# Decoding w_out by ScalarE's product and scaling it by row sums, with a new order of the first batches and of the last tiles

## The chip, the cores and the metric

The kernel runs on one core of one Trainium2 chip. The metric is the time on the device in microseconds (us). A core has TensorE (PE in the profile; PEld is its weight load), VectorE (DVE), ScalarE (ACT), GpSimd (POOL) and SyncE (SP), which here only issues DMAs. Every engine works through its own instructions in program order.

## The reference

There are 8 batches of 8 heads, 576 positions and 64 columns per head, with 32 memory slots per head:

```
a      = softmax(phi over the sequence)
k_m    = a^T k ;  v_m = a^T v                       # 32 memory rows per head
x      = softmax(q k_m^T / 8) v_m                   # 4608 tokens x 512
g      = s * relu(x @ w_in)^2 + b                   # 512 -> 2048
x      = g @ w_out                                  # 2048 -> 512
h      = x @ w_in2                                  # 512 -> 1024
solu   = h * softmax(h)
out    = (solu - mean) / sqrt(var + 1e-6) * g_ln @ w_out2
```

`w_in`, `w_out` and the two second-layer weights arrive as float64. The kernel reads each number as two 32-bit words and makes the float32 itself: three exponent bits of the high word are dropped, the mantissa is moved up by three bits, and the top three bits of the low word are put below it. Products run on TensorE in pairs of float16 parts (hi and lo, three passes), so each tensor needs a power-of-two scale that keeps the hi part in range.

## The kernel before, in words

The work of batch 0, all decoding and splitting of the first-layer weights, and the start of batch 1 are issued in an order written out by hand, the string `FIRST`. Each word is a step: a name, and after the dot its indices. The same order holds on each engine for the instructions that the step puts there, so the string sets what stands behind what on DVE, ACT, POOL, PE and the SP queue. After it a loop runs batches 1 to 7 (gemm1, gemm2, with the next batch's attention in between), and a last loop runs the second layer over 36 tiles of 128 tokens.

The steps that matter here are these. `w_in` and `w_out` come in eight pieces each (chunk c, half x), of 128x1024 numbers. `Lw` and `Lo` load a piece. `Ai` and `Ao` (line 228) let ACT write the absolute value of the high words to the destination. `Bi` and `Bo` (line 238) are a DVE pass that raises each value to at least 2^-15 and writes the row's maximum out as its accumulator. `Ci` and `Co` are two DVE instructions: a shift with a mask (line 254), and a scalar_tensor_tensor that puts two high bits back (line 245). The low bits are put in either by DVE alone (`PiX`, `PoX`, line 1094), or by POOL (`Pi`, `Po`, line 251) after ACT (`LiA`, `LoA`, line 233) or DVE (`LiD`, `LoD`, line 235) has shifted the low word.

For each of the four chunks of `w_out` the row maxima become one scale: `om` reduces them on DVE, `oad` puts them on a diagonal (DVE, line 170), `oap` multiplies it by ones on PE, `oa` reduces that on DVE (line 180), and `os` makes the power of two. The product of `oap`, like those of `vap` and `map`, takes one of the two PSUM tiles with the tag "y", the ones that gemm2's `ya` and `yb` write. Then `xh` (ACT) and `xl` (DVE, line 280), or `xhP` (two ACT instructions) and `xlP` (POOL, line 1163), write the hi and lo parts. `ya.jd` and `yb.jd` are the two halves of gemm2 of batch 0 (block j, output chunk d; 24 products each).

`g.jp` is gemm1 of batch 0 (12 products for two of the 16 blocks of d_ff), `gr` its relu on ACT (line 953). Its square is done by ACT (`gq`, line 978) or POOL (`gqP`, line 980), the hi part by ACT (`gh`, line 970) or DVE (`ghD`, a cast), the lo part by DVE or POOL (`gl`, `glP`, line 985). `s0` to `s6` and `sT` are the scores of the attention; of these `s5` is a DVE subtraction and `s5P` the same on POOL. Batch 1's queries are loaded (`Lq`) into the space in which the decoded `w_out` pieces lay (`wt_s`), so they wait for the last `xl` or `xlP` that reads it. `qa` and `qs` find their scale (lines 274 and 746), `qh` and `ql` split them, `qT` and `mT` transpose them by DMA, and then PE can run `s0.10` (line 780).

In the last loop one round takes gemm3 of tile i (`tile_mm`, line 1335), the solu of tile i with the float16 parts of tile i-1 (`tile_rest`), and gemm4 of tile i-3 (line 1417). gemm4 needs `lt`, a DMA transpose of the tile's normalised values. The result goes out in two DMAs per tile where a tile crosses a column group (line 1427).

## Time and profile before

| | us |
|---|---|
| median of 3 runs | 1139.3 (1137.97 to 1140.17) |
| the profiled execution, its own time | 1138.68 |
| the profiled execution, span of its instructions | 1136.9 |

| engine | busy us | share of the span | instructions |
|---|---|---|---|
| PE | 1060.9 | 93% | 8208 |
| PEld | 691.5 | 61% | 8208 |
| DVE | 804.7 | 71% | 1551 |
| ACT | 517.8 | 46% | 745 |
| POOL | 242.2 | 21% | 181 |

All times in the profile come from that one execution and count from the start of its span. A busy share is an average over stages that have different limits, so it has to be read stage by stage. An instruction's time includes what it spends waiting inside the engine after it has started.

### The profile page before, as it was taken

How to read it: one execution, taken by the hardware profiler on the slowest of the kernel's cores; microseconds unless marked ns; L12 is line 12 of the kernel's file. 1: busy time of each engine (PE TensorE's matmuls, PEld its weight loads, DVE VectorE, ACT ScalarE, POOL GpSimd, SP SyncE). 2: the span in 40 equal slices, each digit the busy share in tenths (PEclk: the TensorE clock that was granted, in tenths of full speed). 3: DMA queues.
4: the chain of work that ended last, by engine and by line, in shares of the span. 5: the costliest groups of instructions: out<-in, count | busy, mean ns of one | idle time of the engine just before them, and what ended most of it. 6: DMA issues, size and time to landing. Idle time of an engine off the chain costs nothing.

```text
span 1136.9 us, 20489 instructions
## 1 busy us (share of the span) xinstructions
PE 1060.9 (93%) x8208; PEld 691.5 (61%) x8208; DVE 804.7 (71%) x1551; ACT 517.8 (46%) x745; POOL 242.2 (21%) x181
## 2 busy tenths in 40 slices
PE   0676799998999999999999999999999999999997
...
DVE  5989977776976776777777675647666666676662
...
GB/s 290 274 142 211 36 80 102 124 217 119 95 186 71 121 166 59 153 134 83 161 142 95 82 26 172 60 47 98 111 101 91 106 109 101 91 108 106 83 64 100
DMA packets 219488, 134.00 MB, mean 118 GB/s; under 512 B 144896, under 2 KB 207616, under 8 KB 219392
## 3 DMA queue, kind: packets, MB, share of 16 engines
...
q0 software_dynamic: 96, 0.01, 0.0%
...
## 4 chain that ended last, share of the span: by engine, by line
PE 69%; DVE 4%; DMA 3%; ACT 2%; SPq 1%; issue 1%; POOL 0%; POOLq 0%; ACTq 0%
PE y L1002 24%; PE hp L1335 16%; PE y L1417 15%; PE hp L942 10%; PE wp L634 2%; PE kp L438 1%; DMA work<-in_moe_w_out_dram 1%; PE sp L780 1%; DVE g L985 1%; DVE wt_s L280 0%; DMA w_in_t<-wt_s 0%; DMA kv_s<-in_k_dram 0%; DMA lt<-nat 0%; SPq L335 0%; DMA qt_s<-work 0%
## 5 line engine op out<-in xcount | busy, mean ns | idle before, releaser
L1002 PE MATMUL y<-g,w_out 128*128 128x288 f16 (+1 forms) x2880 | 366.0, 287 | 5.3 <-DVE first L180 5.3
L1002 PEld LDWEIGHTS <-w_out 128*128 128x128 f16 x3072 | 298.2, 98 | 98.6 <-issue 18.6
L942 PE MATMUL hp<-aT,vwt 128*128 128x288 f16 x1536 | 198.5, 290 | 7.5 <-ACT r L953 4.1
L1417 PE MATMUL y<-w_t,lt 128*128 128x512 f16 x864 | 192.0, 379 | 1.8 <-DMA lt<-nat 1.8
L1335 PE MATMUL hp<-w_t,xs 128*128 128x512 f16 x864 | 192.2, 379 | 0.0
L942 PEld LDWEIGHTS <-vwt 128*128 128x128 f16 x1536 | 151.5, 99 | 51.3 <-issue 9.3
L1417 PEld LDWEIGHTS <-lt 128*128 128x128 f16 x864 | 84.4, 98 | 103.8 <-DMA lt<-nat 2.2
L1335 PEld LDWEIGHTS <-xs 128*128 128x128 f16 x864 | 84.5, 98 | 101.4
L1379 POOL TENSOR_TENSOR rstd<-ve,nhalf 128x1 f32<-128x1 f32 x36 | 52.7, 1464 | 335.8 <-DVE mv L1377 335.8
L1349 DVE TENSOR_REDUCE hmx<-hp 128x1 f32<-128x1024 f32 x36 | 44.1, 1224 | 86.6 <-PE hp L1335 86.6
L277 ACT ACTIVATE xs<-xt,xsc 128x512 f16<-128x512 f32 x36 | 25.9, 720 | 151.0 <-PE hp L1335 129.6
L1019 ACT ACTIVATE x<-y,bcol,cs 128x288 f32<-128x288 f32 x64 | 37.5, 586 | 122.7 <-PE y L1002 101.5
L985 DVE TENSOR_TENSOR g<-r,g 128x576 f16<-128x576 f32 x115 | 88.9, 773 | 6.3 <-POOL r L980 2.5
L978 ACT ACTIVATE r<-r 128x576 f32<-128x576 f32 x118 | 80.6, 683 | 19.4 <-DVE g L985 15.2
L953 ACT ACTIVATE r<-hp 128x576 f32<-128x576 f32 x120 | 77.1, 643 | 13.2 <-PE hp L942 5.7
L274 DVE TENSOR_REDUCE xmx<-x 128x1 f32<-128x288 f32 x64 | 28.7, 448 | 54.1 <-ACT x L1019 53.4
L928 DVE CAST g<-r 128x576 f16<-128x576 f32 x112 | 51.4, 459 | 19.4 <-ACT r L978 19.4
L1356 ACT ACTIVATE e<-hp,nm,xiv 128x1024 f32<-128x1024 f32 x36 | 43.3, 1203 | 46.5 <-DVE nm L1351 46.5
L856 POOL TENSOR_TENSOR e<-e,ssm 96x512 f32<-96x512 f32 x21 | 22.0, 1046 | 186.0 <-DVE ssm L851 183.9
L1425 ACT ACTIVATE o<-y,io 128x512 f32<-128x512 f32 x36 | 24.8, 689 | 51.6 <-issue 43.2
L1393 DVE TENSOR_TENSOR nat<-so,nat 128x1024 f16<-128x1024 f32 x36 | 43.7, 1215 | 5.4 <-ACT nat L1388 5.4
L1372 DVE BATCH_NORM_STATS2 bs<-so 128x6 f32<-128x512 f32 x72 | 46.3, 685 | 1.2
...
## 6 DMA issues: line engine op xcount, KB each, us to landing
...
```

The costliest lines, as they stand in the source:

```text
L928: nc.vector.tensor_copy(out=g_of(n, j, 0)[:, 2 * fp:2 * fp + 2, 0:BLK], in_=gt["r2", j, fp])
L942: nc.tensor.matmul(out=hp[:, u, 0:BLK], lhsT=vt[:, pw, R, f * 128:(f + 1) * 128], rhs=aT[:, CJ * j:CJ * (j + 1), pa, R, :], start=(x == 0) ...
L953: nc.scalar.activation(out=r, in_=gt.pop(("h", j, fp))[:, :, 0:BLK], func=ACTF.Relu, scale=scale)
L978: nc.scalar.activation(out=r2, in_=r, func=ACTF.Square)
L985: (nc.vector if eng == "D" else nc.gpsimd).tensor_tensor(out=g_of(n, j, 1)[:, fs, 0:BLK], in0=gt.pop(("r2", j, fp)), in1=g_of(n, j, 0)[:, ...
L1002: nc.tensor.matmul(out=y[:, 0:w], lhsT=w_out_t[d][:, pw, f, :], rhs=g_of(n, j, pg)[:, f, 0:w], start=(x == 0), stop=(x == len(steps) - 1),)
L1335: nc.tensor.matmul(out=hp[:, a, :], lhsT=xs[:, px, kk, :], rhs=wt[:, pw, kk, a * 512:(a + 1) * 512], start=(kk == 0 and px == 0 and pw == ...
L1349: nc.vector.tensor_reduce(out=mx, in_=hv, op=ALU.max, axis=AX)
L1372: nc.vector.bn_stats(out=bs[:, a, :], in_=so[:, a * 512:(a + 1) * 512])
L1379: nc.gpsimd.tensor_tensor(out=rstd, in0=ve, in1=nhalf, op=ALU.pow)
L1393: nc.vector.tensor_tensor(out=nat[:, 1, :], in0=so, in1=nat[:, 0, :], op=ALU.subtract)
L1417: nc.tensor.matmul(out=y[:, 0:DM], lhsT=lt[:, pl, f, :], rhs=wt[:, pw, f, :], start=(x == 0), stop=(x == len(steps) - 1),)
```

## The change

Four things are changed. First, `w_out` is decoded in another way. `Ao` is now a product on ACT, the high word read as float32 times 2^-112, which keeps the sign and moves the exponent so that a plain shift by three (first instruction of `Co`) leaves the right one; the second instruction of `Co` puts the sign back. [...] Second, `Bo` is no longer a DVE pass: it is an ACT pass over the decoded piece that writes the sum of absolute values of each row as its accumulator, with the used-up high words as its output. The scale is made from the largest of four such sums (two chunks at a time), so `om`, `oad`, `oap`, `oa` and `os` exist twice instead of four times, and `os` no longer decodes the maximum but copies the inverse scale to two columns. Third, `FIRST` is a new order, in which some steps also run on another engine: 4 of the 8 pieces of `w_in` get their low bits by `PiX` (2 before), one of the others by `LiD`; six `ghD` replace one; `gl` is 7 (5 before) and `glP` 9 (11); `gq` 8 (6) and `gqP` 8 (10); `s5` 1 (4) and `s5P` 5 (2). Fourth, in the last loop gemm3 and the solu of the last tile are issued one gemm4 earlier, and the second output DMA of the last tile is issued by ACT's queue instead of SP's.

```diff
+REBIAS = 2.0 ** -112
 FIRST = """
-Lw.01 Lphi.0 Lw.10 Ai.10 phm.0 pht.0 Lw.00 phd.0 Ai.00 Lw.11 pho.0 Bi.10 Lw.30 phb.0 Ci.10 Bi.00 Ai.01 Lw.20 Ai.11
-Lkv.00 LiA.10 Pi.10 Lkv.02 Bi.01 LiA.30 Lkv.01 Bi.11 phe.0 Ci.11 LiA.11 Ai.20 LiA.20 km.00 Ci.00 Ci.01 Lkv.03 Ai.30
-Lw.31 Bi.30 Lw.21 PiX.00 km.01 Bi.20 im0 ks.00 Ci.30 Ci.20 PiX.01 Lq.01 ks.01 LiA.31 Lq.02 Lq.03 Pi.11 Lq.00 Pi.30
-Ai.31 ko.00 ko.01 Bi.31 vb.0 ia0d mm.0 qm.01 Ai.21 vad.0 mv.0 vap.0 Bi.21 Pi.20 LiA.21 qo.01 ia0p va.0 Lphi.1 im
-Ci.31 iad qm.02 mk.0 qm.03 Ci.21 qm.00 phm.1 qo.02 qo.03 ia0 qo.00 iap s0.00 Lo.01 s1.00 s0.01 ia s2.00 Ao.01 pht.1
-Pi.31 s0.02 vs0 s3.00 s1.01 phd.1 s2.01 s3.01 Lo.10 s6P.00 iv s4.00 Lo.00 s6P.01 vm.00 s5.00 vh.00 vm.01 s4.01 s1.02
-s5P.01 sT.00 vl.00 vh.01 pho.1 vl.01 Pi.21 s2.02 sT.01 Ao.00 Lo.11 phb.1 Lo.20 vs.0 vm.03 vh.03 vm.02 Bo.00 vh.02
-vl.03 g.03 Lkv.11 vl.02 s3.02 Bo.01 Lkv.10 g.01 Ao.11 om.0 LoA.10 s6P.02 Ao.10 gr.01 gh.01 Co.01 gr.03 g.07 gqP.03
-Bo.11 gqP.01 g.06 phe.1 gh.03 gl.01 gr.07 glP.03 gqP.07 gr.06 gh.07 km.10 g.05 gq.06 Co.00 gh.06 Co.11 ks.10 s4.02
-glP.07 gr.05 PoX.01 gh.05 gqP.05 g.02 s5.02 oad.0 Lkv.12 Bo.10 sT.02 oap.0 ko.10 gr.02 Lkv.13 oa.0 g.00 os.0 om.1
-gl.05 gr.00 Co.10 gh.02 PoX.00 oad.1 gh.00 xh.00 xh.01 g.11 oap.1 gl.06 oa.1 xl.00 gqP.02 Lo.21 km.11 gq.00 gr.11
-g.13 Ao.20 LoD.11 os.1 ks.11 xl.01 Po.11 Lo.30 gh.11 Lkv.22 Lphi.2 Lkv.21 Ao.21 Po.10 Bo.20 ko.11 Bo.21 om.2 glP.02
-Co.21 vb.1 gr.13 glP.00 g.10 gh.13 gqP.13 g.04 g.16 vad.1 xhP.11 xh.10 gq.11 Lo.31 glP.13 oad.2 oap.2 gr.10 gr.04
-Co.20 xl.10 PoX.20 g.14 glP.11 xlP.11 gh.04 vap.1 gh.10 gq.04 gqP.10 oa.2 ya.01 PoX.21 Ao.30 glP.04 os.2 Ao.31 gr.16
...
+Lw.01 Lw.20 Lphi.0 Lw.10 phm.0 Ai.20 Lkv.00 pht.0 Ai.01 Bi.20 Lw.00 Ai.10 Bi.01 phd.0 pho.0 phb.0 Bi.10 Ci.20 Ci.10
+phe.0 Lw.11 Ci.01 Lw.30 LiA.10 Ai.11 Ai.00 Bi.11 Lkv.02 Pi.10 Bi.00 im0 Lkv.01 Lkv.03 km.00 km.01 Ai.30 Lq.02 ks.01
+Lw.31 Lq.03 Lq.00 Ci.11 ks.00 LiD.11 PiX.01 Bi.30 PiX.20 Lq.01 qm.02 ko.00 Ai.31 ko.01 qo.02 Ci.00 Lphi.1 Ci.30
+Lw.21 Lkv.10 qm.03 qo.03 mm.0 mv.0 qm.00 Bi.31 vb.0 ia0d qo.00 Lo.01 mk.0 qm.01 qo.01 phm.1 s0.01 vad.0 ia0p LiA.00
+s1.01 Ai.21 vap.0 s2.01 Bi.21 Pi.11 s0.00 s3.01 Pi.00 s1.00 va.0 pht.1 ia0 s2.00 s0.02 s6P.01 Lo.00 phd.1 im s4.01
+s5P.01 s3.00 vs0 vm.01 s6P.00 vm.00 Ci.21 iad sT.01 LiA.21 iap s4.00 s5P.00 vh.01 vh.00 s1.02 s2.02 vl.01 ia Ao.00
+pho.1 sT.00 Pi.21 LoA.01 vl.00 phb.1 vm.02 iv Lkv.11 s3.02 Ao.01 vs.0 Lo.11 s6P.02 PiX.30 g.02 vh.02 g.00 gr.02
+vl.02 s4.02 gqP.02 ghD.02 gr.00 Lo.10 Ci.31 gh.00 Co.01 s5.02 Ao.11 sT.02 gq.00 PiX.31 g.03 g.05 gr.03 glP.02 Co.00
+Co.11 gqP.03 Po.01 phe.1 km.10 gl.00 gh.03 g.04 gl.03 gr.05 gq.05 ks.10 Ao.10 ko.10 ghD.05 LoD.11 Po.11 gr.04 g.11
+Lkv.12 Bo.00 gl.05 Lkv.13 Co.10 PoX.10 gr.11 Bo.01 Bo.11 Bo.10 om.0 g.14 vm.03 oad.0 km.11 gh.04 gqP.04 Lo.21 Lo.30
+glP.04 vh.03 PoX.00 oap.0 oa.0 gr.14 gh.14 g.01 gq.11 os.0 gh.11 gqP.14 ks.11 vl.03 xh.01 g.07 ko.11 g.13 gl.11
+xhP.00 gr.01 xh.10 gq.01 xl.10 g.06 xl.01 gh.01 gr.07 xlP.00 gh.07 gl.01 glP.14 g.16 gr.13 LoD.30 gqP.07 Lkv.22
+Lo.31 vb.1 vad.1 Ao.21 vap.1 Ao.30 gq.13 xh.11 Co.30 Lo.20 g.12 ghD.13 gl.07 xl.11 glP.13 Ao.20 Co.21 Ao.31 gr.06
+Po.30 gr.16 mb.1 gqP.16 g.17 mad.1 gq.06 map.1 Bo.30 Co.31 Bo.21 Bo.31 g.10 gh.16 ghD.06 Co.20 Bo.20 om.1 va.1 oad.1
+Lphi.2 oap.1 ma.1 glP.06 oa.1 os.1 PoX.21 gr.12 glP.16 PoX.20 gqP.12 xhP.20 ya.01 xh.21 ya.00 PoX.31 xh.30 xhP.31
+xlP.20 xl.30 yb.01 xlP.31 Lq.10 gr.10 g.15 cb.1 gh.10 yb.00 ghD.12 xl.21 yo.01 glP.12 qa.10 ym.01 phm.2 vs.1 gr.17
+gq.10 cb.0 pha.2 yo.00 Lq.12 gh.17 Lq.11 ya.02 ym.00 ya.03 Lq.13 qa.13 qa.12 yb.02 qa.11 qs.1 yd.01 qh.11 yd.00
+qh.10 ms.1 cb.2 mm.1 mv.1 mh.1 gr.15 yb.03 ql.10 yo.02 ql.11 qT.11 gqP.15 qT.10 ym.02 cb.3 yo.03 glP.10 vm.11 qh.12
+ghD.15 ml.1 gq.17 ym.03 glP.17 qh.13 ql.12 ya.11 gl.15 qT.12 phbP.2 vm.10 vh.11 ql.13 vh.10 yb.11 vl.11 yo.11 qT.13
+mT.1 ya.13 s0.10 Lkv.20 vl.10 ym.11 yb.13 sc.10 s0.11 yd.03 s1.10 ya.10 vm.12 s2.10 sc.11 s3.10 yd.02 yo.13 s6.10
...
 """
@@ -255,6 +257,22 @@
             out=out_, in0=in_, scalar1=3, scalar2=0x3FFFFFF8,
             op0=ALU.logical_shift_left, op1=ALU.bitwise_and,
         )
+
+
+
+    def decode_rebias(dst, raw):
+        nc.scalar.activation(out=dst, in_=raw[:, :, :, 1].bitcast(FP32), func=ACTF.Copy, scale=REBIAS)
+
+    def decode_shift(dst, raw):
+        di = dst.bitcast(I32)
+        nc.vector.tensor_scalar(out=di, in0=di, scalar1=3, scalar2=None, op0=ALU.logical_shift_left)
+        nc.vector.scalar_tensor_tensor(
+            out=di, in0=raw[:, :, :, 1], scalar=-0x80000000, in1=di, op0=ALU.bitwise_and, op1=ALU.bitwise_or,
+        )
+
+
+    def decode_sum(dst, raw, sm):
+        nc.scalar.activation(out=raw[:, :, :, 1].bitcast(FP32), in_=dst, func=ACTF.Abs, accum_out=sm)
 
     def word_max(pk):
 
@@ -1066,27 +1084,31 @@
             return w_in_dst(c, x), raw_t["in", c, x]
         return words(wt_t[c, x]), raw_t["out", c, x]
 
+    def piece_max(c, x):
+        if "i" not in pk_t:
+            pk_t["i"] = st.tile([128, 8], FP32, tag="pk8", name="pk", bufs=2)
+        decode_max(piece("i", c, x)[0], pk_t["i"][:, 2 * c + x:2 * c + x + 1])
+
+    def piece_sum(c, x):
+        if c // 2 not in pk_t:
+            pk_t[c // 2] = st.tile([128, 4], FP32, tag="pk4", name="pk", bufs=2)
+        col = 2 * (c % 2) + x
+        decode_sum(*piece("o", c, x), pk_t[c // 2][:, col:col + 1])
+
     def piece_abs(w, c, x):
         if w == "o":
             at = (2 * c + x) % 4
             wt_t[c, x] = wt_s[:, at] if at < 3 else flat(kv_s[:, 2])[:, 0:1024]
-        decode_abs(*piece(w, c, x))
+        (decode_abs if w == "i" else decode_rebias)(*piece(w, c, x))
 
     def piece_low(w, c, x, eng):
         decode_low(raw_t["in" if w == "i" else "out", c, x], eng)
 
-    def piece_max(w, c, x):
-        key, col, n = ("i", 2 * c + x, 8) if w == "i" else (c, x, 2)
-        if key not in pk_t:
-            pk_t[key] = st.tile([128, n], FP32, tag=f"pk{n}", name="pk", bufs=2)
-        decode_max(piece(w, c, x)[0], pk_t[key][:, col:col + 1])
-
     def piece_bits(w, c, x):
-        decode_bits(*piece(w, c, x))
+        (decode_bits if w == "i" else decode_shift)(*piece(w, c, x))
 
     def piece_add(w, c, x):
         decode_add(*piece(w, c, x))
-        raw_t.pop(("in" if w == "i" else "out", c, x))
 
 
     def piece_or(w, c, x):
@@ -1095,7 +1117,6 @@
             out=dst.bitcast(I32), in0=raw[:, :, :, 0], scalar=29, in1=dst.bitcast(I32),
             op0=ALU.logical_shift_right, op1=ALU.bitwise_or,
         )
-        raw_t.pop(("in" if w == "i" else "out", c, x))
 
     def w_max(key):
         pk_t["m", key] = word_max(pk_t[key] if key == "i" else pk_t.pop(key))
@@ -1138,14 +1159,14 @@
         nc.vector.tensor_scalar(out=s22, in0=sb[:, 0:1], scalar1=2.0 ** 22, scalar2=None, op0=ALU.mult)
 
     def w_out_scale(d):
-        mx = st.tile([128, 1], FP32, tag="wmx", name="wmx")
-        word_value(pk_t.pop(("m", d)), mx)
-        pk_t["s", d] = pow2_scale(mx, iw[:, d:d + 1], "wsc")
+        inv = st.tile([128, 1], FP32, tag="winv", name="winv")
+        pk_t["s", d] = pow2_scale(pk_t.pop(("m", d)), inv, "wsc")
+        nc.vector.tensor_copy(out=iw[:, 2 * d:2 * d + 2], in_=inv.to_broadcast([128, 2]))
 
     def w_out_ops(d, x):
         sl = slice(8 * x, 8 * x + 8)
         t = wt_t[d, x].rearrange("p (k d) -> p k d", k=8)
-        return w_out_t[d][:, 0, sl], w_out_t[d][:, 1, sl], t, pk_t["s", d]
+        return w_out_t[d][:, 0, sl], w_out_t[d][:, 1, sl], t, pk_t["s", d // 2]
 
     def w_out_hi(d, x, eng):
         hi, lo, t, sc = w_out_ops(d, x)
@@ -1423,8 +1444,9 @@
             )
         o = pools_b["o"].tile([128, DM], FP32, tag="o", name="o")
         nc.scalar.activation(out=o, in_=y[:, 0:DM], func=ACTF.Copy, scale=io2[:, 0:1])
-        for off, n, bb, c, p in runs(i * 128, 128):
-            nc.sync.dma_start(out=out_v[bb, c, p:p + n, :], in_=o[off:off + n, :])
+        for x, (off, n, bb, c, p) in enumerate(runs(i * 128, 128)):
+            eng = nc.scalar if i == NTILE - 1 and x else nc.sync
+            eng.dma_start(out=out_v[bb, c, p:p + n, :], in_=o[off:off + n, :])
 
 
     def load_w_in0(f, kp):
@@ -1460,7 +1482,7 @@
         "Ai": lambda c, x: piece_abs("i", c, x), "Ao": lambda c, x: piece_abs("o", c, x),
         "LiA": lambda c, x: piece_low("i", c, x, "A"), "LoA": lambda c, x: piece_low("o", c, x, "A"),
         "LiD": lambda c, x: piece_low("i", c, x, "D"), "LoD": lambda c, x: piece_low("o", c, x, "D"),
-        "Bi": lambda c, x: piece_max("i", c, x), "Bo": lambda c, x: piece_max("o", c, x),
+        "Bi": piece_max, "Bo": piece_sum,
         "Ci": lambda c, x: piece_bits("i", c, x), "Co": lambda c, x: piece_bits("o", c, x),
         "Pi": lambda c, x: piece_add("i", c, x), "Po": lambda c, x: piece_add("o", c, x),
         "PiX": lambda c, x: piece_or("i", c, x), "PoX": lambda c, x: piece_or("o", c, x),
@@ -1503,15 +1525,13 @@
         def tile_rest(i):
 
 
-            if i < NTILE:
-                solu_1(i, *h3_t.pop(i))
-            if 1 <= i <= NTILE:
+            solu_1(i, *h3_t.pop(i))
+            if i:
                 solu_3(i - 1)
             if i == NTILE - 1:
                 solu_4(i - 1)
-            if i < NTILE:
-                solu_2(i)
-            if 1 <= i <= NTILE and i != NTILE - 1:
+            solu_2(i)
+            if i and i != NTILE - 1:
                 solu_4(i - 1)
 
         h3_t = {}
@@ -1543,17 +1563,25 @@
                     x_max(n // 2)
                     xal_t[n // 2] = all_max(xal_t[n // 2], "xal")
 
+
         for i in range(2, NTILE + 3):
-            if 3 <= i < NTILE:
+            if 3 <= i < NTILE - 1:
                 tile_mm(i)
             if i == 6:
                 x_max(3)
                 xal_t[3] = mm_max_put(xal_t[3])
             if i == 9:
                 xal_t[3] = mm_max(xal_t[3])
-            tile_rest(i)
+            if i < NTILE - 1:
+                tile_rest(i)
+            if i == NTILE - 2:
+                tile_mm(i + 1)
+                tile_rest(i + 1)
             if i >= 3:
                 gemm4(i - 3)
+            if i == NTILE - 1:
+                solu_3(i)
+                solu_4(i)
 
 
 # ---- launch: one core; inputs and outputs as the reference has them ----
```

## Rows read from the trace of the kernel before

**Rows 1.** The page's 40 slices of the span (28.4 us each), busy tenths of PE and DVE.

```profile
PE   0676799998999999999999999999999999999997
DVE  5989977776976776777777675647666666676662
```

**Rows 2.** Windows: start:end, length, busy time of PE, PEld, DVE, ACT, POOL, granted clock.

```profile
11.10:122.20 111.10, 61.76 (x668) 42.89 (x669) 104.93 (x167) 60.37 (x75) 51.21 (x27) 0.88 0.79 215
122.30:136.60 14.30, 14.27 (x96) 10.44 (x96) 14.02 (x23) 6.24 (x8) 8.30 (x5) 0.83 0.08 22
136.60:144.10 7.50, 5.23 (x31) 3.60 (x30) 7.36 (x15) 0.98 (x2) 4.24 (x3) 0.79 0.19 59
```

**Rows 3.** Timeline of PE: start, length, line, count, in brackets idle time and releaser.

```profile
122.33 14.46 PE L1002 MATMUL y<-g,w_out 128*128 128x289 f16 x96 [5.28 <-DVE first L180]
...
136.62 1.63 PE L942 MATMUL hp<-aT,vwt 128*128 128x288 f16 x12
140.53 0.46 PE L175 MATMUL mp<-first 128*128 128x128 f32 x2 [2.27 <-DVE first L170]
...
144.06 3.27 PE L1002 MATMUL y<-g,w_out 128*128 128x289 f16 x24
...
169.83 0.86 PE L780 MATMUL sp<-work 128*96 128x64 f16 x16 [1.07 <-DMA work<-work]
```

**Rows 4.** DVE instructions by line and form until 122.2 us: busy, mean ns, idle before.

```profile
L238 DVE TENSOR_SCALAR_CACHE_REDUCE w_in_t<-w_in_t 128x1024 f32<-128x1024 f32 x8 | 9.6, 1213 | 0.2 <-ACT w_in_t L228 0.2
...
L238 DVE TENSOR_SCALAR_CACHE_REDUCE wt_s<-wt_s 128x1024 f32<-128x1024 f32 x5 | 6.0, 1197 | 0.0
L254 DVE TENSOR_SCALAR w_in_t<-w_in_t 128x1024 int32<-128x1024 int32 x8 | 5.7, 718 | 0.0
...
L245 DVE SCALAR_TENSOR_TENSOR w_in_t<-raw_g,w_in_t 128x1024 int32<-128x1024 int32 x2 | 2.5, 1225 | 0.1
...
L1094 DVE SCALAR_TENSOR_TENSOR w_in_t<-raw_v,w_in_t 128x1024 int32<-128x1024 int32 x2 | 2.4, 1214 | 0.0
```

**Rows 5.** The page's costliest groups over the whole span: two that FIRST uses too.

```profile
L985 DVE TENSOR_TENSOR g<-r,g 128x576 f16<-128x576 f32 x115 | 88.9, 773 | 6.3 <-POOL r L980 2.5
...
L928 DVE CAST g<-r 128x576 f16<-128x576 f32 x112 | 51.4, 459 | 19.4 <-ACT r L978 19.4
```

**Rows 6.** Timeline of DVE, single instructions of the first 160 us.

```profile
11.09 0.69 DVE L360 TENSOR_TENSOR t<-phi_sb 96x512 f32<-96x512 f32 x1 [9.46 <-DMA phi_sb<-in_phi_dram]
...
22.99 0.96 DVE L254 TENSOR_SCALAR w_in_t<-w_in_t 128x1024 int32<-128x1024 int32 x1
...
25.85 3.31 DVE L245 SCALAR_TENSOR_TENSOR w_in_t<-raw_v,w_in_t 128x1024 int32<-128x1024 int32 x1
...
119.92 2.16 DVE L1094 SCALAR_TENSOR_TENSOR wt_s<-w_out,wt_s 128x1024 int32<-128x1024 int32 x1
122.00 0.28 DVE L180 TENSOR_REDUCE first<-mp 128x1 f32<-128x128 f32 x1
...
153.42 0.14 DVE L746 TENSOR_REDUCE qm<-qmx 96x1 f32<-96x4 f32 x1
```

**Rows 7.** Timeline of POOL beside the third of these.

```profile
25.34 2.73 POOL L251 TENSOR_TENSOR w_in_t<-w_in_t,raw_g 128x1024 int32<-128x1024 int32 x1 [1.94 <-ACT raw_g L233]
```

**Rows 8.** Timeline of ACT: two first passes over loaded pieces, and an accumulator read-out.

```profile
13.64 1.12 ACT L228 ACTIVATE w_in_t<-raw_g 128x1024 f32<-128x1024 f32 x1 [11.63 <-DMA raw_g<-in_moe_w_in_dram]
...
26.05 1.13 ACT L228 ACTIVATE w_in_t<-raw 128x1024 f32<-128x1024 f32 x1 [1.13 <-DMA raw<-in_moe_w_in_dram]
...
1070.83 0.19 ACT L1356 ACTIVATION_READ_ACCUMULATOR e<-hp,nm,xiv 128x1 f32 x1
```

**Rows 9.** Timelines of PE, DVE and SP's queue at the end.

```profile
1109.40 15.70 PE L1417 MATMUL y<-w_t,lt 128*128 128x512 f16 x72
1126.86 5.35 PE L1417 MATMUL y<-w_t,lt 128*128 128x512 f16 x24 [1.76 <-DMA lt<-nat]
...
1109.60 1.22 DVE L1349 TENSOR_REDUCE hmx<-hp 128x1 f32<-128x1024 f32 x1 [2.63 <-PE hp L1335]
...
1133.01 0.79 SPq L1427 DMA_DIRECT2D out_dram<-o  x2
```

12 lines of the change are left out of this document (3 added, 9 removed).

## The prediction, on record before the changed kernel ran

> **What bounds the kernel now.** I read the page's slices first: from slice 6 on PE is full to the end, so the 0.9 ms of batches and second layer can only get shorter by less PE work, and the change takes none away there. Lost time lies in the first five slices, where DVE is the full row and PE the one with holes [rows 1]. The windows say the same in numbers: from 11.1 to 122.2 us DVE is busy for 104.9 of 111.1 us, PE for 61.8, ACT for 60.4, POOL for 51.2; up to 144.1 DVE stays full and PE runs at a granted clock near 0.8 [rows 2]. Third the timeline of PE: gemm2 (`ya.01`) starts at 122.33 when a DVE reduction, `oa.2`, has read one of the two "y" tiles of PSUM; the last hole that DVE makes is the 2.27 us ahead of 140.53; at 144.06 `ya.02` starts, and from there PE has work behind it, but for 1.07 us at `s0.10`, which waits for a DMA transpose [rows 3]. So the head is a DVE stage that ends at a gate, and what the change is worth there is how much sooner PE comes to the state it now has at 144.06. Last the end: PE waits 1.76 us for the last tile's transpose before the last gemm4, and two output DMAs are then issued one behind the other [rows 9].
>
> **The gate moves.** In the new order `ya.01` stands behind `map.1` and `oap.1`, so its "y" tile is free when DVE has done `ma.1`. All eight `Co` and all row sums come before that; in the old order six `Co` did. I therefore count DVE's work ahead of `oa.2` (old) and of `ma.1` (new).
>
> Less: six `Bo` passes of 1.2 us [rows 4], 7.2. More: two `Co`, each a 0.7 us shift and a 1.2 us merge [rows 4], 3.8; one merge of low bits in sum (`PiX` 2 to 4, `PoX` 3 to 2), 1.2; two shifts of low words (`LiD`, `LoD`: 1 to 3), taken at the 0.7 of the other shift, 1.4; four `ghD` at 0.46 [rows 5], 1.8; three `gl` at 0.77, 2.3. One `s5` and half a dozen instructions of 0.14 to 0.28 [rows 6] go in sum with one scale chain less, about 1.5, an estimate. Sum: -7.2 + 3.8 + 1.2 + 1.4 + 1.8 + 2.3 - 1.5 = +1.8 us. The gate has more DVE work before it, not less; the two `Bo` and the work left out behind it (over all of `FIRST` DVE loses two more `Bo` and a second scale chain) come back only after the gate.
>
> **The start.** `phm.0` is DVE's first step of weight and waited for phi until 11.09 [rows 6]. phi stood second in SP's queue, behind one 1 MB piece; now it stands third, behind two. The piece that stood right behind phi came at 13.64, 2.55 us later [rows 8]; the seventh transfer came at 26.05, five pieces behind phi, 3.0 us each. I take +2.6, ends +2.0 and +3.0. What DVE does in the order after that (`Bi.20`, `Bi.01`) has its data by then: these two pieces are now ahead of phi.
>
> **POOL beside DVE.** The merge that starts at 25.85 takes 3.31 us where the same form takes 1.2, and ends 1.1 us after POOL's add from 25.34 to 28.07: it waited for POOL's instruction to end [rows 6, 7, 4]. 18 DVE instructions before the gate are lengthened like this, the first at 22.99 (0.96 for 0.69), the last at 119.92 (2.16 for 1.21), in sum by 20 us. With 51.2 us of POOL that is 0.39 us per us. The passes of line 238 are not among them: 8 and 5 of them average 1.21 and 1.20 [rows 4]. The new order has 23 POOL instructions ahead of the gate for 26, which alone gives 20 x 23/26 = 17.7; but six of the fourteen passes beside which POOL ran for nothing are gone. POOL was busy 46% of the stage [rows 2], so 7.2 us of passes covered 3.3 us of it. 17.7 + 3.3 x 0.78 (2.1 lost in 2.73 of POOL, as at 25.85) = 20.3: no change. Ends: 17.7, and 0.78 x 45 us of POOL = 35. I stay at 20, the mean of the 18.
>
> The Trainium skill, page "SBUF — State Buffer", section "Who interferes with whom", says that DVE and GpSimd share a pair of ports as an exclusive lock, that a `tensor_scalar` which also writes out its accumulator does not take it, and that a plain one, or one with two inputs in SBUF, can. By that rule the change removes just those DVE instructions that were free of POOL; the trace agrees (1.20 and 1.21 beside 3.31). By the rule all 3.3 us would turn into waiting, and the gate would be 0.7 us later than by my sum.
>
> **ACT.** Eight sums come to ACT. A pass over a piece takes 1.12 and the read-out of an accumulator 0.19 [rows 8]: 1.3 us each, and three `LiA` and five `gh` go. ACT has 51 us free before the gate [rows 2], so the sum costs nothing; what can cost is its order. Two places: `xl.10` on DVE waits for `xh.10`, which stands behind `xh.01`, the two instructions of `xhP.00` and `gr.01`, some 5.0 us after `os.0`, while DVE has about 2.6 us of other work: 2.4 us of stall. And `om.1` needs `Bo.20`, which needs the last `Co`: 1.3 us at least, 3.7 if `Bo.31` and `gh.16` are still ahead of it. Behind both everything on DVE is queued, and PE behind that. Together 2.4 + 1.5 = 3.9, of which part falls into time that POOL's lock costs anyway; of the 6.2 us of old idle time [rows 2] I expect 2.3 to go (the new order does DVE work where it waited for squares). Net +1.6, ends -2.5 and +5.
>
> **The sum at the head.** Gate: 122.3 + 1.8 + 2.6 + 0 + 1.6 = 128.3. Behind it the four halves `ya.01`, `ya.00`, `yb.01`, `yb.00` took 14.3 us at clock 0.83 [rows 2, 3]; at the 3.0 or so of a half at 144.06 they would take 12. I take 13.2. But between 136.6 and 144.06 PE did two `g` blocks and two small products and stood idle for 2.27; in the new order these are done before the gate. So `ya.02` comes at 141.5 instead of 144.06: -2.5. It has to find its data: `xlP.20` is done some 10 to 11 us after the gate, in time. Next late is `s0.10`: the chain from `qs` (153.42) to it (169.83) took 16.4 us [rows 6, 3], through six DMA transposes and ACT. In the new order I reckon `qs` at about 152, so `s0.10` can run at about 168.4 and PE gets there at about 168. It fits, with nothing to spare.
>
> **The end.** gemm3 of the last tile ends one gemm4 (15.70/3 = 5.2) sooner, at about 1104.4. Its chain from there to the transposed tile took 1126.86 - 1109.60 = 17.3; DVE is still at the solu of the tile before for some 2.5 us more. 1124.2, and PE is through the others at 1109.40 + 15.6 = 1125.0: the wait of 1.76 goes, ends 0 and -1.8. The second output DMA no longer stands behind the first: half of 0.79 [rows 9], -0.4, ends 0 and -0.4. Together -2.2.
>
> **Sum.** -2.5 - 2.2 = -4.7 us against the profiled execution's own 1138.68 (span 1136.9 and 1.8 around it): 1134.0. The median of the runs is 0.6 above that execution: 1134.6.
>
> **Rivals.** (a) *DVE is starved or blocked more*: the price of POOL rises to 0.6 us per us, since merges and shifts now follow each other without a free pass between. Place: DVE between `vl.00` and `ma.1`; price 27 instead of 20 and another 0.5 us or so at `om.1`, gate at 135.8. For it: the rows at 25.85 and 119.92; against it: three POOL instructions fewer. It decides from a gate later than 133.0: 144.06 less 13.2 is 130.8, and the end gives 2.2. Time: 1134.6 + 7.5 = 1142.1, slower than before. This is the lock that the Trainium skill describes on its page "SBUF — State Buffer", section "Who interferes with whom". (b) *The queries' chain holds `s0.10`* where it was, at 169.83: PE has one half less and one `vm` more done there, 1.0 us less work, so the head turns from -2.5 to +1.0 and only the end is left: 1139.3 - 2.2 + 1.0 = 1138.1. For it: PE already waits there for a transpose; against it: the work ahead of `qs` is less by the last scale chains. (c) *The order overlaps better than I count*: POOL at 17.7, no stalls at `xl.10` and `om.1`: gate 128.3 - 2.3 - 3.9 = 122.1, time 1128.4 if the queries keep pace. For it: over all of `FIRST` DVE has some 8 us less to do; against it: both stalls follow from the order of the steps. (d) That the end doesn't gain, because the last tile's chain is late by the same time, would add 1.8 to any of these.
>
> **Chances.** Forecast (1131.5 to 1137.5) 0.50, (a) 0.15, (b) 0.20, (c) 0.15. About 0.2%, 2.3 us, can be told from no change here: faster is below 1137.0, slower above 1141.6. Of the forecast 0.46 lies below 1137.0, (c) wholly, of (b) 0.04 below and the rest in between, (a) above but for 0.01. Faster 0.65, same 0.20, slower 0.15. The range from 1129 to 1140.5 leaves out most of (a) and the far part of (c).
>
> **What would show it.** No DVE instruction of line 238 on `wt_s` and eight ACT passes with a read-out; `phm.0` near 13.7; `ya.01` near 128.3 with the two stalls of DVE ahead of it, released by ACT; no hole in PE from there to `s0.10`; `s0.10` near 168; no wait ahead of the last gemm4. Wrong it is if DVE's lengthened instructions before the gate sum to much other than 20 us, if PE has a hole of over 1 us behind the gate, or if the last gemm4 still waits.

## The result, and the profile after

The changed kernel takes 1146.99 us (1146.11 to 1148.35) against 1139.3: a ratio of 1.0071 [1.0057, 1.0084] (in brackets, here and below, the 95% interval). It is slower, and the forecast was faster. The profiled execution's span grew from 1136.9 to 1145.2.

The page's slices of PE, DVE and the granted clock:

```profile
PE   0586589998999999999999999999999999999998
DVE  4998877767776876876776776637666666666662
PEclk9788899999999999999999999999999999999999
```

Against [rows 1], with slices counted from 0, PE has lost a tenth in slice 1, gained one in slice 2, and lost two in slice 4 and one in slice 5 (114 to 172 us); from slice 6 on nothing differs but the last digit, so the loss lies in the first 172 us. The windows follow (columns as in [rows 2]; behind the granted clock stand, there too, the busy share of the DMA engines and GB/s): from phi's landing to the gate, the gate to `ya.02`, `ya.02` to `s0.10`, and on to batch 1's first product.

```profile
15.88:135.70 119.82, 69.47 (x691) 46.33 (x692) 108.25 (x162) 64.16 (x86) 48.80 (x26) 0.83 0.69 185
136.10:150.60 14.50, 14.50 (x110) 11.05 (x108) 9.90 (x15) 9.29 (x11) 6.75 (x4) 0.92 0.08 22
150.60:181.26 30.66, 25.41 (x188) 17.45 (x186) 23.00 (x45) 10.90 (x17) 9.64 (x7) 1.00 0.38 83
181.26:203.69 22.43, 22.43 (x185) 15.39 (x184) 14.52 (x24) 10.13 (x14) 4.31 (x4) 0.92 0.37 97
```

PE's timeline, the rows that answer to [rows 3] and [rows 9]:

```profile
136.12 10.21 PE L1020 MATMUL y<-g,w_out 128*128 128x289 f16 x72
146.16 1.63 PE L960 MATMUL hp<-aT,vwt 128*128 128x288 f16 x12
147.64 6.12 PE L1020 MATMUL y<-g,w_out 128*128 128x289 f16 x48
155.06 6.12 PE L1020 MATMUL y<-g,w_out 128*128 128x289 f16 x48 [1.30 <-ACT x L1037]
...
168.13 0.28 PE L1020 MATMUL y<-q_s,w_out 128*128 128x288 f16 x1 [1.65 <-POOL q_s L1003]
...
181.26 0.86 PE L798 MATMUL sp<-work 128*96 128x64 f16 x16 [2.30 <-DMA work<-work]
...
1104.15 10.52 PE L1356 MATMUL hp<-w_t,xs 128*128 128x512 f16 x48
1114.51 26.06 PE L1438 MATMUL y<-w_t,lt 128*128 128x512 f16 x120
```

The gate is at 136.12, 13.8 us later than in [rows 3]. `ya.02`, the second half of the 48 at 147.64, is at 150.7: +6.6. Then three holes follow, 1.30, 1.65 and 2.30 us, where before had one of 1.07 us, and `s0.10` is +11.4; batch 1's first product (96 matmuls of `hp`) starts at 203.69 for 192.68, +11.0. At the end five gemm4s run in one piece, the wait of [rows 9] is gone, and from batch 1's first product to the end of the span 2.7 us come back: +8.3 in the span.

DVE's timeline: the instructions up to the gate that waited for more than 1 us, one (94.83) that took 2.90 us beside GpSimd where the form takes 0.69, and two behind the gate:

```profile
15.88 0.69 DVE L378 TENSOR_TENSOR t<-phi_sb 96x512 f32<-96x512 f32 x1 [14.25 <-DMA phi_sb<-in_phi_dram]
22.09 1.75 DVE L428 TENSOR_TENSOR phi_sb<-phi_sb,tx 96x1536 f32<-96x1536 f32 x1 [1.26 <-PE tx L408]
50.74 2.50 DVE L378 TENSOR_TENSOR t<-phi_sb 96x512 f32<-96x512 f32 x1 [1.94 <-DMA phi_sb<-in_phi_dram]
94.83 2.90 DVE L268 TENSOR_SCALAR wt_s<-wt_s 128x1024 int32<-128x1024 int32 x1
102.40 0.16 DVE L280 TENSOR_REDUCE first<-pk 128x1 f32<-128x4 f32 x1 [1.32 <-ACT w_out L275]
108.19 0.16 DVE L495 TENSOR_SCALAR rs<-kp 128x1 f32<-128x1 f32 x1 [1.88 <-PE kp L481]
111.21 3.81 DVE L298 SCALAR_TENSOR_TENSOR w_out<-wt_s,sc,w_out 128x1024 f16<-128x1024 f32 x2 [1.60 <-ACT w_out L295]
134.93 0.16 DVE L280 TENSOR_REDUCE first<-pk 128x1 f32<-128x4 f32 x1 [1.27 <-ACT w_out L275]
...
158.34 0.15 DVE L764 TENSOR_REDUCE qm<-qmx 96x1 f32<-96x4 f32 x1
...
172.92 4.19 DVE L298 SCALAR_TENSOR_TENSOR kv_s<-wt_s,sc,kv_s 96x768 f16<-96x768 f32 x1
```

GpSimd's row beside the one at 94.83:

```profile
94.39 2.79 POOL L253 TENSOR_TENSOR kv_s<-kv_s,raw 128x1024 int32<-128x1024 int32 x1 [6.78 <-issue]
```

The longest wait of DVE between phi's landing and the gate in the kernel before:

```profile
81.03 1.78 DVE L985 TENSOR_TENSOR g<-r,g 128x576 f16<-128x576 f32 x1 [2.46 <-POOL r L980]
```

The two rows of line 280 are `om.0` and `om.1`, which wait for the row sums (L275 on ACT); 111.21 is `xl.10`, 158.34 belongs to `qs.1`, 172.92 is `ql.13`. Line 238's pass on `wt_s` [rows 4] has gone, and ACT shows eight passes of 1.12 to 1.17 with a read-out of 0.18 to 0.20, as priced from [rows 8].

Single traces of one head differ: a kernel with the head of before unchanged (the first experiment) has its gate at 123.84 and batch 1's first product at 194.90. So differences of up to 2.2 us between two traces are not read here; the ratios decide.

### The profile page after: what moved, and what is told of

The parts are those of the page before. It is cut to its first block, busy times and chain, and to the rows that moved or that the text cites. A ratio compares the mean times of both kernels' runs of the same rounds, so it can differ in the third digit from the quotient of the medians.

```text
span 1145.2 us, 20448 instructions
## 1 busy us (share of the span) xinstructions
PE 1064.5 (93%) x8204; PEld 691.9 (60%) x8204; DVE 796.5 (70%) x1521; ACT 521.4 (46%) x755; POOL 237.3 (21%) x179
## 4 chain that ended last, share of the span: by engine, by line
PE 75%; DVE 11%; DMA 6%; ACT 3%; issue 2%; SPq 2%; POOL 1%; ACTq 0%; DVEq 0%; POOLq 0%
PE y L1020 27%; PE y L1438 16%; PE hp L1356 16%; PE hp L960 11%; DMA kv_s<-in_k_dram 2%; PE wp L652 1%; PE kp L456 1%; PE sp L798 1%; DVE g L1003 1%; DMA raw<-in_moe_w_in_dram 1%; SPq L355 1%; DVE wt_s L268 1%; DMA w_in_t<-wt_s 1%; DVE wt_s L298 1%; DMA work<-in_moe_w_out_dram 1%
```

## The experiments

Theory at first: the time follows DVE's line up to the gate, and the change lengthened that line by late loads and by the order of its steps. Rival: the sums on ACT stand in its in-order queue between DVE's `Co` and the relus that PE waits for. All edits below are moves in `FIRST` unless shown otherwise; each ratio is to the kernel before, run beside it. The last two columns are the start of `ya.01` (the gate) and of batch 1's first product, in us, in the one profiled execution of each kernel; those of e2 and e7 were 2.1 and 3.4 us faster than the median of their runs.

| run | what it is | us | ratio | gate | batch 1 |
|---|---|---|---|---|---|
| e1_end | before + new end | 1138.16 | 0.9985 [0.9976, 0.9994] | 123.84 | 194.90 |
| e2_decode | before + new decode, a scale per chunk | 1142.71 | 1.0024 [1.0014, 1.0034] | 124.57 | 194.79 |
| e5_late | e2, sums later | 1139.52 | 1.0008 [0.9999, 1.0017] | 123.79 | 193.82 |
| e6_nosum_old | e2 without the sums | 1135.10 | 0.9974 [0.9964, 0.9984] | 120.67 | 188.47 |
| e8_best | e5 + new end + three moves | 1135.97 | 0.9971 [0.9960, 0.9982] | 122.05 | 191.22 |
| e11_fill | e8 + `Co` into a hole | 1133.73 | 0.9953 [0.9940, 0.9965] | 120.11 | 189.88 |
| e12_philate | before, phi third | 1144.11 | 1.0043 [1.0029, 1.0057] | 127.69 | 198.62 |
| e3_loads | changed, phi second | 1142.53 | 1.0029 [1.0018, 1.0039] | 132.42 | 198.70 |
| e4_tail | changed, moves behind the gate | 1148.82 | 1.0083 [1.0069, 1.0098] | 135.55 | 204.96 |
| e7_nosum_new | changed without the sums | 1143.18 | 1.0037 [1.0023, 1.0050] | 131.04 | 196.46 |
| e9_loads_nosum | e3 without the sums | 1140.37 | 1.0013 [1.0002, 1.0024] | 128.85 | 195.88 |
| e10_perchunk | e3, a scale per chunk | 1148.42 | 1.0078 [1.0062, 1.0093] | 128.15 | 204.65 |
| e13_cbfirst | e10, `cb.0 yo.00` earlier | 1143.47 | 1.0037 [1.0024, 1.0051] | 127.57 | 200.71 |
| e14_phi2 | e13, second phi later | 1137.03 | 0.9980 [0.9971, 0.9989] | 126.74 | 193.78 |
| e15_two | e3, second phi later | 1138.63 | 0.9994 [0.9985, 1.0004] | 131.85 | 194.84 |

**e1_end: the end alone.** Before, with the diff's `tile_rest`, loop and output DMAs.

> The kernel before with the new end alone (gemm3 and the solu of the last tile one gemm4 earlier, the second output DMA of the last tile on ACT's queue). Both theories of the head: 1.8 us of waiting ahead of the last gemm4 go and 0.4 us of DMA issue, so 1137.1 against 1139.3, no wait for lt, nothing else in the trace moved. If the end of the changed kernel costs instead, 1139 to 1142.

Measured 0.9985: 0.7 to 2.7 us less, which holds the 2.2 expected. As in the changed kernel, the five gemm4s run in one piece (`1095.34`, then 120 matmuls).

**e2_decode: the decode alone.**

```diff
- Bo.00 ... Bo.01 ... om.0 ... Co.01 ... Bo.11 ... Co.00 ... Co.11 ... oad.0
+ Co.01 Bo.01 ... Co.00 Bo.00 ... Co.11 Bo.11 ... om.0 oad.0
```

> The old order and the old end with the new decode of w_out (ACT's product, ACT's row sums behind each Co), one scale per chunk as before. Theory 'order' (the decode is sound, the new order and the scale for two chunks lose the time): DVE loses eight passes of 1.2 us, gemm2 starts 3 to 7 us sooner than 122.3, time 1133 to 1137. Theory 'decode' (the passes that went were free of POOL's lock and the sums on ACT come too late, so the decode itself costs): gemm2 starts at 124 or later, time 1141 to 1146.

It is slower, though DVE is busy for 95.2 us up to 122.2 where before it was 105.75. The timelines of ACT and PE of this kernel show why:

```profile
112.09 1.13 ACT L275 ACTIVATE raw<-wt_s 128x1024 f32<-128x1024 f32 x1 [3.90 <-DVE wt_s L269]
113.11 0.18 ACT L275 ACTIVATION_READ_ACCUMULATOR raw<-wt_s 128x1 f32 x1
114.94 1.12 ACT L275 ACTIVATE w_out<-wt_s 128x1024 f32<-128x1024 f32 x1 [1.64 <-DVE wt_s L269]
115.96 0.18 ACT L275 ACTIVATION_READ_ACCUMULATOR w_out<-wt_s 128x1 f32 x1
116.04 0.73 ACT L971 ACTIVATE r<-hp,relu 128x576 f32<-128x576 f32 x1
```

```profile
116.82 3.04 PE L960 MATMUL hp<-aT,vwt 128*128 128x288 f16 x12 [7.45 <-ACT r L971]
```

ACT stood still for 3.90 and 1.64 us ahead of two sums whose data DVE had not written; the relu at 116.04 was queued behind, and PE waited 7.45 us for it. So DVE's saving was paid back through ACT. That speaks for the rival; e6 below prices it.

**e3_loads and e4_tail: loads and order in the changed kernel.**

```diff
- Lw.01 Lw.20 Lphi.0 Lw.10 phm.0 Ai.20 Lkv.00 ...
+ Lw.01 Lphi.0 Lw.20 Lw.10 phm.0 Ai.20 ... Lw.30 Lkv.00 ...
```

```diff
- xhP.20 ... xh.30 ... phm.2 vs.1 ... pha.2 ... qs.1 ... qh.11 ... gr.15 ... phbP.2 ... ql.13
+ xh.30 xhP.20 ... qs.1 phm.2 vs.1 pha.2 ... gr.15 qh.11 ... ql.13 phbP.2
```

> The changed kernel, with phi loaded second again and the first k and v behind the weights, as before. If the late phi (15.9 us instead of 11.1) is what the head pays for, DVE starts 4 to 5 us sooner, the gate moves by as much and the time is 1142 to 1143. If DVE then only waits for its pieces of weights, phi at 11 to 12 but the gate stays within 1.5 us of 136.1 and the time within 1.5 of 1147.0.

> The changed kernel with four moves behind the gate: xh.30 ahead of xhP.20 on ACT; gr.15 ahead of qh.11 on ACT; phm.2 and vs.1 on DVE (and pha.2 on POOL) behind qs.1; phbP.2 on POOL behind ql.13. If the order behind the gate loses what the runs show there (gemm1 of batch 1 starts 11.0 us late, 5 of them at ya.02, 6 behind it), the holes of 1.3, 1.65 and 2.3 us on PE shrink and the time is 1141 to 1143.5. If these holes are only the late gate passed on, PE waits elsewhere by as much and the time stays at 1146 to 1148.

e3 came as expected: phi lands at 11.14, the gate comes 3.7 us earlier and the ratio falls by 0.0042. e4 is a miss. PE's waits only changed place: the all-reduce `pha.2` on GpSimd came later with `phm.2`, and PE's wait for GpSimd's `q_s` rose from 1.65 to 5.8 us, PE's row in e4:

```profile
170.72 0.40 PE L1019 MATMUL y<-q_s,w_out 128*128 128x288 f16 x1 [5.78 <-POOL q_s L1002]
```

**e5_late, e6_nosum_old, e7_nosum_new: the sums moved, and left out.** e5 also has `xl.10` ahead of `om.2` and chunk 3's sums behind `yo.01`; e6 and e7 are e2 and the changed kernel with the second edit, which also takes away DVE's wait for the sums.

```diff
- Co.00 Bo.00 gh.06 Co.11 Bo.11 ... gr.05 gh.05 ... Co.10 Bo.10 gh.02 ... Co.21 Bo.21 Co.20 Bo.20 vb.1 gr.13 ...
+ Co.00 gh.06 Bo.00 Co.11 ... gr.05 gh.05 Bo.11 ... Co.10 gh.02 Bo.10 ... gr.13 gh.13 xhP.11 xh.10 gq.11 Co.21 Bo.21 Co.20 Bo.20 vb.1 ...
```

```diff
-        nc.scalar.activation(out=raw[:, :, :, 1].bitcast(FP32), in_=dst, func=ACTF.Abs, accum_out=sm)
+        nc.vector.memset(sm, 18.0)
```

> The order and the end of the kernel before with the new decode and a scale per chunk (1142.7 when the sums stood right behind each pass that they read); here ScalarE's sums stand behind the relus and copies that TensorE waits for, and the sums of chunk 2 behind the split of chunk 1. Theory 'the sums hold up ScalarE's queue': the 7.45 us wait of PE for r at 116.8 and the 4.2 us wait of DVE for the split of chunk 1 at 120.8 go, batch 1's first product (the 96 hp matmuls) starts 4 to 7 us earlier than 194.8, time 1136 to 1139. Rival 'the decode's passes themselves cost it': the waits change place and the time stays at 1141 to 1143.

> The same kernel of 1142.7 us with the eight sums left out (the scale's input is a constant 18.0, so the scale isn't computed from the data). It prices the sums: theory 'the sums hold up ScalarE's queue': 1134 to 1138, below the kernel before, since the eight passes of 1.2 us that were maxima on DVE are gone and nothing stands in their place. Rival 'the product and the shift cost it': 1140 to 1143.

> The changed kernel whole, with only the eight sums left out (the scale's input is a constant 18.0, so the scale isn't computed from the data). Theory 'the late loads and the order of the steps make the changed kernel slow': the sums' waits at om.0 and om.1 go (1.3 us each), so 1143 to 1146, still slower than before. Rival 'the sums on ScalarE make it slow': 1138 or less.

Place alone is worth 0.0016 (e5 against e2, with intervals that overlap a little), the sums as a whole 0.0050 (e6 against e2). In e5 PE's 7.45 us for the relu are gone, but neither the gate nor the first product moved by more than two traces differ, since PE now waits for the bound of chunk 2 on DVE:

```profile
119.90 0.80 PE L177 MATMUL mp<-first 128*128 128x128 f32 x2 [10.48 <-DVE first L172]
```

So e5 is a half-hit: the time missed its range by 0.5 us, and the first product did not come 4 to 7 us earlier. In the changed kernel the sums are worth 0.0034, and without them it is still slower than before (1.0037). Both theories hold, each for a part.

**e8_best and e11_fill: placing what is left.** Both have the diff's new end, too.

```diff
- glP.07 gr.05 PoX.01 ... om.0 oad.0 ...   xl.10 om.2 oad.2 ...   xlP.21 yo.01 Bo.30 Bo.31
+ glP.07 gr.05 om.0 oad.0 PoX.01 ...   om.2 oad.2 xl.10 ...   xlP.21 Bo.30 Bo.31 yo.01
```

```diff
- Co.01 Bo.01 gr.03 g.07 ... gl.01 ... gq.06 Co.00 gh.06 Bo.00 Co.11
+ Co.01 Bo.01 Co.00 Co.11 gr.03 g.07 ... gl.01 ... gq.06 gh.06 Bo.00
```

> The kernel with the order of before, a scale per chunk and the sums placed late (1139.5), with the changed kernel's end (-1.3 when it stood alone) and three more moves: the bounds of chunk 0 and of chunk 2 go ahead of DVE work that nothing waits for (om.0 oad.0 ahead of PoX.01, om.2 oad.2 ahead of xl.10), and chunk 3's two sums go ahead of yo.01, into a stretch in which ScalarE waited 3.5 us. Theory 'placement decides': the 10.5 us wait of PE for first at 119.9 shrinks by about 3, the gate comes at 120 to 121 instead of 123.8, batch 1's first product at about 190 instead of 193.8, time 1134 to 1137, below both kernels. Rival 'what the sums cost can't be placed away': 1138 or more.

> The kernel of 1135.97 us (order of before, late sums, the changed end) with the shift passes of chunks 0 and 1 (Co.00 Co.11) placed into the 5.1 us in which DVE waits for GpSimd's r at 76.9 to 82.0, instead of behind it. Theory 'the DVE's order before the gate sets the time': the wait at 82.0 shrinks to under 1.5, the gate comes 2 to 4 us before 122.05, time 1132.5 to 1135. Rival 'what follows waits for loads and relus anyway': 1135 to 1136.5.

Both times lie in the ranges of the theory, and both kernels beat the two of this case; their marks fell somewhat short (e8's gate at 122.05 for 120 to 121, e11's wait 2.07 us for under 1.5). e11's edit is two steps moved into a hole; DVE's timeline of e8, then of e11:

```profile
82.01 1.78 DVE L1003 TENSOR_TENSOR g<-r,g 128x576 f16<-128x576 f32 x1 [5.12 <-POOL r L998]
```

```profile
82.81 1.78 DVE L1003 TENSOR_TENSOR g<-r,g 128x576 f16<-128x576 f32 x1 [2.07 <-POOL r L998]
87.09 0.16 DVE L280 TENSOR_REDUCE first<-pk 128x1 f32<-128x2 f32 x1 [2.50 <-ACT w_out L275]
```

3.0 us of the wait is filled; 2.5 us come back at `om.0`, which now waits for ACT's sum. The ratio falls by 0.0018, with intervals that just overlap, and the gate is 1.9 us earlier, which alone could be the difference of two traces.

**e12_philate: the late load alone, in the kernel before.**

```diff
- Lw.01 Lphi.0 Lw.10 Ai.10 phm.0 ...
+ Lw.01 Lw.10 Lphi.0 Ai.10 phm.0 ...
```

> The kernel before with one edit: phi's load goes third instead of second on the queue, behind Lw.01 and Lw.10, as it does in the changed kernel. Theory 'phi's late landing is a cost of its own': phi lands at 15 to 16 instead of 11.1, DVE's first work and with it the gate (122.33) and batch 1's first product (192.68) come 3 to 5 us later, time 1142 to 1144.5. Rival 'DVE makes it up before the gate': within 1 us of before.

DVE's first row and PE's gate of this kernel:

```profile
16.30 0.69 DVE L360 TENSOR_TENSOR t<-phi_sb 96x512 f32<-96x512 f32 x1 [14.67 <-DMA phi_sb<-in_phi_dram]
```

```profile
127.69 2.57 PE L1002 MATMUL y<-g,w_out 128*128 128x289 f16 x10 [5.45 <-DVE first L180]
```

phi is 5.2 us later than in [rows 6], the gate 5.4, and the ratio is 1.0043 (4.9 us). DVE makes none of it up.

**e9_loads_nosum and e10_perchunk.** e9 is e3 with the memset shown above. e10 is e3 with `pk`, `w_out_scale` and `w_out_ops` per chunk as before, and chunk 3 behind the gate:

```diff
- ... Co.30 ... Bo.30 Co.31 Bo.21 Bo.31 ... om.1 ... ya.01 xh.21 ya.00 PoX.31 xh.30 xhP.31 ... yo.01 ...
+ ... om.2 ... xhP.20 Co.30 Co.31 ya.01 xh.21 Bo.30 Bo.31 Po.30 ya.00 ... yo.01 om.3 oad.3 oap.3 oa.3 os.3 PoX.31 xh.30 xhP.31 xl.30 xlP.31 ...
```

> The changed kernel with both repairs at once: phi's load second again (alone -4.2 us against the changed kernel) and the eight sums left out (alone -3.4 to -3.8; the scale's input is a constant 18.0, so the scale isn't computed from the data). If the two costs are apart from each other, about 1138 to 1140; the order and the end of before with the decode and no sums stood at 1135.1, so what is left above 1134 (its value with the new end) is the new order of steps. If phi's delay and the sums' waits lie beside each other, no better than 1141.

> The changed kernel with phi's load second again (1142.5) and a scale per chunk instead of one for two chunks, so that chunk 3's shift passes (4 of some 0.7 and 1.2 us, with locks about 5.5 us), sums and bound stand behind the gate. Theory 'two chunks at a time puts chunk 3 ahead of the gate': gate 4 to 6 us before 132.4, batch 1's first product 2 to 5 us before 198.7, time 1138 to 1141. Rival: the work only moves behind the gate and delays ya.03 and the queries' chain as much: 1142 to 1144.

In e9 the costs add up only in part: with phi second the sums are worth 0.0016, with intervals that overlap. e10 is a miss in time and a hit at the gate: 4.3 us earlier than e3's, and 0.0049 slower. The next runs ask where that went.

**e13_cbfirst, e14_phi2, e15_two: behind the gate.**

```diff
- ym.01 phm.2 vs.1 gr.17 gq.10 cb.0 pha.2 yo.00 ...
+ ym.01 cb.0 yo.00 phm.2 vs.1 gr.17 gq.10 pha.2 ...
```

```diff
- phm.2 vs.1 ... pha.2 ... qh.13 ql.12 ... phbP.2 ... s0.10 Lkv.20 ... s2.10 ...
+ vs.1 ... qh.13 phm.2 ql.12 ... s0.10 Lkv.20 pha.2 ... s2.10 phbP.2 ...
```

e15 makes the second of these moves in e3, with `gr.15` ahead of `qh.11`.

> The kernel of 1148.4 us (changed kernel, phi second, a scale per chunk, gate at 128.15) with cb.0 and yo.00 ahead of phm.2 on DVE and ScalarE. Theory 'the gate's gain was lost in the queue behind phm.2 and vs.1': PE's wait of 7.9 us for x at 153.3 falls under 2.5, batch 1's first product at 198 to 200 instead of 204.65, time 1141 to 1143.5. Rival: the queries' chain holds the next product whatever ya.02 does, 1146 or more.

> The kernel of 1143.5 us (changed kernel, phi second, a scale per chunk, cb.0 and yo.00 ahead) with the three steps of the second phi (phm.2, pha.2, phbP.2) at their places of before: behind qh.13, behind Lkv.20, behind s2.10. Theory 'they are too early: GpSimd stands in the all-reduce from 155.4 until its next piece at 164.4, and PE waits 6.6 us for it': that wait goes, batch 1's first product at 194 to 197 instead of 200.7, time 1137.5 to 1140.5. Rival 'the chain of the queries is what holds it': 1142 to 1144.

> The changed kernel with phi's load second (1142.5) and its scale for two chunks kept, with the second phi's three steps at their places of before and gr.15 ahead of qh.11. Theory as for the run beside it: batch 1's first product at 194 to 197 instead of 198.7, time 1138 to 1141; if 'two chunks at a time' costs on its own, this stands 1 to 3 us above the run beside it, otherwise within 1.

The three moves pay as the theory had it, e14 by somewhat more than its range (1137.0 for 1137.5 to 1140.5), and e13's first product comes 0.7 us behind its range. What the recorded texts call the second phi is the phi of batch 2. PE's timeline of e10, and of e13 with GpSimd's beside it:

```profile
153.34 3.06 PE L1020 MATMUL y<-g,w_out 128*128 128x289 f16 x12 [7.89 <-ACT x L1037]
```

```profile
147.07 7.78 PE L1020 MATMUL y<-g,w_out 128*128 128x289 f16 x48 [2.20 <-ACT x L1037]
166.78 0.40 PE L1020 MATMUL y<-q_s,w_out 128*128 128x288 f16 x1 [6.63 <-POOL q_s L1003]
```

```profile
155.38 1.08 POOL L417 PARTITION_ALL_REDUCE px<-pm  x1 [5.75 <-DVE ex L213]
156.34 0.39 POOL L528 MEMSET work<- 128x256 f32 x1
164.35 1.14 POOL L998 TENSOR_TENSOR r<-r 128x576 f32<-128x576 f32 x1 [7.62 <-issue]
```

In e10 the product that waits is `ya.03`: it needs the PSUM tile that `yo.00` reads, `yo.00` needs `cb.0`, and `cb.0` stands on DVE behind `phm.2`. In e13 that wait is 2.20, but GpSimd shows nothing from 156.7 to 164.35 behind the all-reduce `pha.2`, and PE waits 6.63 us for `glP.10`, which is queued there behind `gqP.15`. With the three steps of batch 2's phi at their old places (e14) the wait is 2.02, `s0.10` comes at 173.02 instead of 179.95, and the ratio falls from 1.0037 to 0.9980. In the changed kernel with its scale for two chunks the same move gives 1.0029 to 0.9994 (e15). PE's waits for GpSimd's `q_s` and for `s0.10` in e3, then what is left of them in e15:

```profile
164.86 0.28 PE L1019 MATMUL y<-q_s,w_out 128*128 128x288 f16 x1 [2.09 <-POOL q_s L1002]
177.94 0.86 PE L797 MATMUL sp<-work 128*96 128x64 f16 x16 [0.58 <-DMA work<-work]
```

```profile
168.39 0.28 PE L1019 MATMUL y<-q_s,w_out 128*128 128x288 f16 x1 [0.85 <-DVE q_s L1002]
174.08 0.86 PE L797 MATMUL sp<-work 128*96 128x64 f16 x16 [0.51 <-DMA work<-work]
```

e14 and e15 ran ten times each beside each other, and e15 is 1.6 us slower. That lies in the 1 to 3 us that were named beforehand as the sign that two chunks at a time cost on their own. But the intervals just overlap, and the two kernels differ in `gr.15` and in the place of chunk 3's steps too, so it speaks for such a cost and does not show it.

## Why the prediction was wrong

Two steps failed: the waits of DVE before the gate, priced at +1.6 and measured at +5.4, with phi's landing mis-sized beside them; and "no hole in PE" from the gate to `s0.10`, where three holes came. The prediction's sum was -4.7 us and the span grew by 8.3. Of the 13.0 us between, 7.8 lie at the gate, about 1.3 from there up to `ya.02`, 4.4 from `ya.02` to batch 1's first product, and -0.5 at the end. By its own terms, from [rows 2] and the first window above:

- **The start, +2.6 (ends +2.0 and +3.0): measured +4.8.** Mis-sized, outside its ends. I took the spacing of pieces that follow each other, 2.55 and 3.0 us [rows 8], as the price of one more piece ahead. What counts is how long phi itself waits: its time from issue to landing was 9.8 us and is 14.1 (the last number of its row in the DMA view of the first 30 us).

```profile
phi_sb<-in_phi_dram SPq DMA_DIRECT2D x1, 576.0 KB, 14.1
```

  The spacing itself was as assumed: the 1 MB piece that now stands ahead is there at 12.78 (ACT's row below), and phi 3.1 us later. But that piece, in second place, lands 1.7 us later than the smaller phi did in second place (11.09).

```profile
12.78 1.12 ACT L230 ACTIVATE w_in_t<-raw 128x1024 f32<-128x1024 f32 x1 [10.77 <-DMA raw<-in_moe_w_in_dram]
```

  e12 shows that all of the delay reaches the gate and the time, e3 that most of it can be undone (the gate comes 3.7 us earlier). Of what made the kernel slower it is the largest single part, 0.0042 of the 0.0071; of the forecast's error only the 2.2 us beyond the +2.6.
- **DVE's work, +1.8: measured +2.9** (108.25 less 20.6 of lengthening, against 104.93 less 20.2). The sign was right, and 1.1 us were missing.
- **GpSimd beside DVE, 0: measured +0.4.** Counted as what instructions took over the shortest of their line and shape, 16 are lengthened by 20.6 us in sum; before it was 18 and 20.2, the list that [rows 6] opens. With one more short instruction the count after is 17 and 21.6, which moves 1 us from the term above to this one. The Trainium skill's page "SBUF — State Buffer", section "Who interferes with whom", says that a plain `tensor_scalar` can contend with GpSimd for the shared ports, and the form that writes out its accumulator does not. Here the shift that takes 0.7 us alone took 2.9 three times beside GpSimd, which agrees. The prediction's step from that rule, 3.3 us more of waiting for the lost accumulator passes, is not seen: the sum hardly moved, beside 48.8 us of GpSimd's work for 51.2. Why is not shown.
- **ACT, "the sum costs nothing", net +1.6 (ends -2.5 and +5): measured +5.4 of DVE idle time.** The two stalls that I named came, together 2.9 us for 3.9 (`xl.10` 1.60 for 2.4, `om.1` 1.27 for 1.5). The old waits went, too, 3.8 us in sum where I had 2.3, among them the 2.46 at 81.03. What failed is that four other waits, 6.4 us in sum, had no term: `om.0` 1.32 for a sum on ACT, `ko.11` 1.88 for PE, 1.26 at `phb.0` for PE, and `phm.1` 1.94 for the phi of batch 1, to which DVE now comes 3.2 us sooner (48.8 for 52.0 us) while its load is issued at 44.6 us as before (44.0). And I priced the sums by ACT's free time. They are in-order work between DVE and the relus: left out, they are worth 0.0016 to 0.0050 by their place (e9, e7, e6).
- **The gate, 128.3: 136.12.** 4.8 + 2.9 + 0.4 + 5.4 = 13.5 after 122.33; the 0.3 that is left lies between DVE's last step and PE, which now does the product of `oap.1` first.
- **Behind the gate, -8.5 up to `ya.02`: measured -7.2.** The four halves took 13.1 us for the 13.2 assumed. The other 1.5 is a block of gemm1, `g.15` (the 12 matmuls at 146.16), which the new order puts between them and I did not count; before, it stood behind `ya.02`.
- **Then +4.4 where I had "no hole":** 1.30, 1.65 and 2.30 us in PE, for the 1.07 of before. From `qs` to `s0.10` it took 22.9 us instead of 16.4. I followed the queries' chain but not what the new order put into its queues: `phm.2` on DVE ahead of `cb.0`, `pha.2` on GpSimd ahead of `gqP.15`, `phbP.2` beside `ql.13` (the row of 4.19 us). This is the second step that failed: 0.0035 (e15 against e3, `gr.15` with it).
- **The end, -2.2: 2.7 in the trace, 0.7 to 2.7 in e1.** The last 168 products of PE took 1.9 us less, as forecast. The -0.4 for the output DMA is not seen: from PE's end to the span's end it took 4.7 us and takes 4.6.

Of the rivals, (a) had the sign and its deciding mark, a gate later than 133.0, but not its cause: the lengthening was 20.6 (21.6 at most) and not 27. (b) had the right place, `s0.10`, but there the chain came later than before and not where it was. In thousandths of the time: +7.1, less 4.2 for phi's load (e3, which puts the first k and v back with it), less 3.5 for the steps of batch 2's phi, gives e15's -0.6, of which -1.5 is the end. What is left of decode, scale for two chunks and order together is about +0.9, and e11 shows that the same decode, in the old order with a scale per chunk and its sums placed by who waits behind them, gives -4.7 with the end. The order as a whole against the old one was not tried step by step.
